# Block-sparse attention with a gated MLP: sums inverted on GpSimd, value products in column halves, K and Q transposed as loaded

## The chip, the cores and the metric

The kernel runs on one core of one Trainium2 chip. The metric is the device time of one execution in microseconds, taken as the median of several runs. The engines are TensorE (PE in the profile, with PEld for its weight loads), VectorE (DVE), ScalarE (ACT), GpSimd (POOL) and SyncE (SP), which issues DMAs.

## The reference

q, k and v have 4 batches, 8 heads, 768 positions and a head size of 64. Positions form 24 blocks of 32. A query block sees itself and its two neighbours, the first and the last block, and three sampled blocks; the first and the last query block see everything.

```python
scores = scale * np.matmul(q, k.transpose(0, 1, 3, 2))
mask = np.abs(blk_i - blk_j) <= window              # window = 1
mask = mask | (blk_i == 0) | (blk_j == 0) | (blk_i == n_blocks - 1) | (blk_j == n_blocks - 1)
# and the three sampled blocks of each query block
scores = np.where(mask, scores, -1000000000.0)
scores = scores - np.max(scores, axis=-1, keepdims=True)
attn = np.exp(scores)
attn = attn / (np.sum(attn, axis=-1, keepdims=True) + 1e-09)
x = np.matmul(attn, v)                              # heads side by side: 3072 tokens x 512
h = x @ w_in                                        # 512 -> 2048
g = h * (1.0 / (1.0 + np.exp(-beta * h)))
out = g @ w_out                                     # 2048 -> 512
```

## The kernel before

**A planner sets the order.** The kernel adds tasks, each with an engine (or several to choose from), an expected duration, dependences and a priority. `plan.run()` plays them through at build time, hands out the eight PSUM banks, and gives one order. The instructions are emitted in it, so each engine works its own list in order, with semaphores between engines. A task with a choice, such as `nrm` with `{"POOL": 1.85, "DVE": 0.8}`, goes where the planner expects it to end first; a bias keeps `nrm` and `gn` mostly on GpSimd.

**Loading.** For batch 0, SyncE loads K, Q and V in float32 and VectorE casts K and Q (L397). For batches 1 to 3, GpSimd issues the loads, which cast on the way, into two raw buffers `RAW`; a raw partition holds six positions for every head, (head, position, dim). VectorE then copies them (`perm`, L447) into (position, head, dim): `K16`, `Q16` and `Vn`. V goes on to a table in DRAM (`VT`), from which the sampled blocks' rows are gathered.

**Transposing.** `trK` and `trQ` (L463) transpose 128x128 pieces, two heads at a time, into a PSUM bank, six for a pair of heads. `evK` and `evQ` copy the bank to `KT` and `QT`: 128 partitions are two heads of 64 dims.

**Pairs of query blocks.** 44 pairs (11 for each batch) go through: `kg` on GpSimd gathers the sampled key blocks (L521), `kn` copies the neighbours on GpSimd or VectorE, `sc` makes the scores of all heads in two banks (L600 for the mask, L610), in tiles of 64 rows by 32 columns of the array; `mx` finds the maxima (VectorE, L621), `ex` the exponentials and their sums (ScalarE, L629). `rc` inverts the four sums (VectorE, L635), `nrm` multiplies (mostly GpSimd, L641), `tp` transposes the weights (L653), `ptv` copies them out (L657), `av` multiplies by the values (L668), and two `xv` tasks copy the result to `xT`.

`av` multiplies two heads' values, 128 columns, with the weights of both heads, 64 columns:

```python
nc.tensor.matmul(
    o[:, (g * NHP + hp) * 64:(g * NHP + hp + 1) * 64],
    lhsT=vgb[:, g, c, hp * P:(hp + 1) * P],
    rhs=pt[:, g, c, :, hp * BLK:(hp + 1) * BLK], ...)
```

So half of each product crosses heads and is not used. Each `xv` takes the useful part of one half: 64 partitions, for the head that stands in them.

**Global rows.** The first and last query blocks of a batch go through similar steps in four rounds: `gs`, `gm`, `ge`, `gr` (sum and reciprocal on VectorE, L733 and L734), `gn` (multiply, L737), `gt`, `gptv`, and then one `gav` for all (L758) with two `gx` copies.

**The MLP.** Eight groups of tokens follow the attention as their blocks come ready: `h` (L817), `tanh` (L823), `stt` (L828), `y` (L845), `oe` (L263) and the store. The planner fills TensorE's gaps with them; after the last pair only MLP work is left.

Of the kernel before, what the change touches and what calls it, by code (L numbers as in the profile page):

```python
# [10 lines left out]
FP32 = mybir.dt.float32  # L11
# [3 lines left out]
ALU = mybir.AluOpType  # L15
# [167 lines left out]
def kernel(  # L183
# [16 lines left out]
    P = 128  # L200
# [20 lines left out]
    ones = sb("ones", [P, P])  # L221
    maskr = sb("maskr", [P, NB - 2, 4])
# [8 lines left out]
    K16 = sb("K16", [P, J, D_MODEL])  # L231
    Q16 = sb("Q16", [P, J, D_MODEL])
    RAW = [sb(f"RAW{i}", [P, H, J * D]) for i in range(2)]
# [33 lines left out]


# [3 lines left out]
    def emit_ident():  # L272
        make_identity(nc, identity)
        nc.gpsimd.memset(ones, 1.0)
    t_ident = add("ident", "POOL", 2.0, emit_ident, prio=-100)
# [110 lines left out]
    for i, (nm, t, dst) in enumerate((("K", k, K16), ("Q", q, Q16), ("V", v, None))):  # L386
        for f in range(2):
            tl = add(f"ld{nm}0.{f}", "SP", 0.47, lambda i=i, t=t, f=f: nc.sync.dma_start(
                out=stage_half(i, f) if i < 2 else v_stage[:, f * HH:(f + 1) * HH, :],
                in_=src6(t, 0, f * HH, HH)), prio=-80 + i * 2 + f, dma=2.0, hw=1)  # L390
            if nm == "V":
                v0ld.append(tl)
                continue
            for hp in range(2 * f, 2 * f + 2):
                ld[nm, 0, hp] = add(
                    f"cast{nm}0.{hp}", "DVE", 0.5,
                    lambda i=i, dst=dst, hp=hp: nc.vector.tensor_copy(  # L397
                        out=dst[:, :, hp * P:(hp + 1) * P].rearrange("p j (h d) -> p h j d", h=2),
                        in_=stage32(i, hp).rearrange("p h (j d) -> p h j d", j=J)),
                    deps=[tl], prio=-72 + 4 * i + hp)  # L400
# [30 lines left out]
    trK, trQ, evK, evQ, vperm, vtab, perm = {}, {}, {}, {}, {}, {}, {}  # L431
    later = {b: [] for b in range(B)}
    for b in range(B):
        pr = prep_prio(b)
        if b:
            vperm[b] = []
            for nm, t, raw, dst in (("V", v, RAW[0], Vn[b % 2]), ("K", k, RAW[1], K16), ("Q", q, RAW[0], Q16)):
                tr = {"K": trK, "Q": trQ}.get(nm)
                for f in range(2):
                    hs = slice(f * HH, (f + 1) * HH)  # L440
                    free = [vperm[b][f]] if nm == "Q" else [perm["QK"["VK".index(nm)], b - 1, f]] if b > 1 else []
                    tl = add(f"ld{nm}{b}.{f}", "POOL", 0.9, lambda t=t, raw=raw, b=b, f=f, hs=hs:
                             nc.gpsimd.dma_start(out=raw[:, hs, :], in_=src6(t, b, f * HH, HH)),
                             deps=free + [t_wout[-1]] if b == 1 else free,
                             prio=(-40 if b == 1 else pr - 30) + "VKQ".index(nm) + 0.5 * f, dma=2.55, bulk=THR)
                    later[b].append(tl)
                    tpm = add(f"perm{nm}{b}.{f}", "DVE", 0.55, lambda raw=raw, dst=dst, hs=hs: copy_on(  # L447
                        "DVE", dst[:, :, hs.start * D:hs.stop * D].rearrange("p j (h d) -> p h j d", h=HH),
                        raw[:, hs, :].rearrange("p h (j d) -> p h j d", j=J)),
                        deps=[tl] + ([tr[b - 1, hp] for hp in range(2 * f, 2 * f + 2)] if tr else []),  # L450
                        prio=pr - 5 * (nm == "V"))
                    if nm == "V":
                        vperm[b].append(tpm)
                    else:
                        perm[nm, b, f] = tpm
                        for hp in range(2 * f, 2 * f + 2):
                            ld[nm, b, hp] = tpm
        for nm, s16, dstT, tr, ev in (("K", K16, KT, trK, evK), ("Q", Q16, QT, trQ, evQ)):
            for hp in range(NHP):
                def emit_tr(nm=nm, s16=s16, b=b, hp=hp):  # L460
                    o = bank16((nm, b, hp))
                    for j in range(J):
                        nc.tensor.transpose(  # L463
                            out=o[:, j * P:(j + 1) * P],
                            in_=s16[:, j, hp * P:(hp + 1) * P],
                            identity=identity)
# [36 lines left out]
    for n, (b, p) in enumerate(order_pairs):  # L503
# [116 lines left out]
        for u in range(2):  # L620
# [14 lines left out]
        rc = add(f"rc{n}", "DVE", 0.09, lambda sb_=sb_: nc.vector.reciprocal(  # L635
            out=sb_[:, 2, :], in_=sb_[:, 1, :]), deps=[ex[n, 0], ex[n, 1]], prio=pr)

        def emit_nrm(eng, pb=pb, sb_=sb_):
            for u in range(2):
                for g in range(2):  # L640
                    (nc.vector if eng == "DVE" else nc.gpsimd).tensor_scalar(  # L641
                        out=pb[:, u, g, :], in0=pb[:, u, g, :],
                        scalar1=sb_[:, 2, 2 * u + g:2 * u + g + 1], scalar2=1.0,
                        op0=ALU.mult, op1=ALU.mult)
        nrm[n] = add(f"nrm{n}", {"POOL": 1.85, "DVE": 0.8}, None, emit_nrm, deps=[rc], prio=pr - 0.5)
# [15 lines left out]
        def emit_av(n=n, vgb=vgb):  # L661
            o = bank(("O", n))
            pt = PT[n % NPT].rearrange("x (g c u m) -> x g c u m", g=2, c=2, u=2)
            first = True
            for g in range(2):
                for hp in range(NHP):
                    for c in range(2):
                        nc.tensor.matmul(  # L668
                            o[:, (g * NHP + hp) * 64:(g * NHP + hp + 1) * 64],
                            lhsT=vgb[:, g, c, hp * P:(hp + 1) * P],  # L670
                            rhs=pt[:, g, c, :, hp * BLK:(hp + 1) * BLK],
                            start=first, stop=(c == 1), skip_group_check=True)
                        first = False
        av[n] = add(f"av{n}", "PE", 0.47, emit_av, deps=[ptv[n], vres] + vg[n], prio=pr - 0.5, lat=0.2,
                    opens=(("O", n),))
        evs = []
        for u in range(2):
            def emit_xv(eng, n=n, u=u, b=b, i0=i0):
                src = bank(("O", n))[u * D:(u + 1) * D, :].rearrange(
                    "x (g h v m) -> x g h v m", g=2, h=NHP, v=2)[:, :, :, u, :]  # L680
                c0 = x_of(b * NB + i0)
                dst = xT[u * D:(u + 1) * D, :, c0:c0 + 2 * BLK].rearrange(
                    "x h (g m) -> x g h m", g=2)
                copy_on(eng, dst, src)
            evs.append(add(f"xv{n}.{u}", {"DVE": 0.42, "ACT": 0.38}, None, emit_xv, deps=[av[n]], prio=pr - 0.5,
                           closes=(("O", n),)))
# [7 lines left out]
    for b in range(B):  # L694
        for w, (blk, u) in enumerate((bl, u) for bl in (0, NB - 1) for u in range(2)):
# [36 lines left out]
            def emit_gr(s_=s_):  # L732
                nc.vector.tensor_reduce(out=s_[:, 5:6], in_=s_[:, 3:5], axis=AX.X, op=ALU.add)  # L733
                nc.vector.reciprocal(out=s_[:, 6:7], in_=s_[:, 5:6])  # L734
            gr = add(f"gr{m}", "DVE", 0.26, emit_gr, deps=[ge], prio=pr)
            gn[m] = add(f"gn{m}", {"POOL": 0.9, "DVE": 0.44}, None, lambda eng, s_=s_, pg=pg: (
                nc.vector if eng == "DVE" else nc.gpsimd).tensor_scalar(  # L737
                out=pg, in0=pg, scalar1=s_[:, 6:7], scalar2=1.0, op0=ALU.mult, op1=ALU.mult),
                deps=[gr], prio=pr)
# [13 lines left out]
        def emit_gav(b=b):  # L753
            o = bank(("GO", b))
            first = True
            for hp in range(NHP):
                for j in range(J):
                    nc.tensor.matmul(  # L758
                        o[:, hp * P:(hp + 1) * P], lhsT=Vn[b % 2][:, j, hp * P:(hp + 1) * P],
                        rhs=PTG[:, j, :, hp * BLK:(hp + 1) * BLK],  # L760
                        start=first, stop=(j == J - 1), skip_group_check=True)
                    first = False
        gavt[b] = add(f"gav{b}", "PE", 1.4, emit_gav, deps=[gptv[gun - 4 + w] for w in range(4)] +
                      vperm[b], prio=pr, lat=0.2, opens=(("GO", b),))
        evs = []
        for u in range(2):
            def emit_gx(eng, u=u, b=b):
                src = bank(("GO", b))[u * D:(u + 1) * D, :].rearrange(
                    "x (h k v m) -> x h k v m", h=NHP, k=2, v=2)
                for kk, blk in enumerate((0, NB - 1)):  # L770
                    c0 = x_of(b * NB + blk)
                    dst = xT[u * D:(u + 1) * D, :, c0:c0 + BLK]
                    copy_on(eng, dst, src[:, :, kk, u, :])
            evs.append(add(f"gx{b}.{u}", {"DVE": 0.55, "ACT": 0.5}, None, emit_gx, deps=[gavt[b]], prio=pr,
                           closes=(("GO", b),)))
# [128 lines left out]
```

## Time and profile before

| | |
|---|---|
| median of 3 runs (lowest to highest) | 323.93 us (323.91 to 328.18) |
| profiled execution, its own time | 323.59 us |
| its span | 321.8 us, 10665 instructions |
| mean granted clock | 0.929 of full |
| PE busy | 280.7 us (87%) in 3525 matmuls |
| PEld busy | 177.3 us (55%) |
| DVE busy | 246.7 us (77%) in 572 instructions |
| ACT busy | 216.8 us (67%) in 644 |
| POOL busy | 187.5 us (58%) in 528 |
| DMA | 43.97 MB in 42211 packets |

The span runs from the first to the last instruction that the profiler saw, and the execution's own time has 1.8 us more. Busy time is the sum over an engine's instructions; for PE the ends of matmuls are modelled, so the distance between two starts tells more than a duration. In a row of a group stand line, engine, operation, output and input with shapes, the count, then busy us and mean ns of one, then the idle time of the engine before them and what ended it.

### The profile page before, as it was taken

What the parts mean: (1) busy time and instruction counts of PE and PEld (TensorE: products, weight loads), DVE (VectorE), ACT (ScalarE), POOL (GpSimd) and SP (SyncE); (2) the same over time, 40 slices, a digit from 0 to 9 for tenths busy, and PEclk for the clock granted to TensorE, in tenths of its full rate; (3) what the DMA queues carried; (4) which work ended last, traced back from release to release, by engine and by line L of the source; (5) the groups of instructions that cost most, each with busy time, mean ns of one, the idle gap of its engine ahead of it and who ended that gap; (6) DMA issues with size and microseconds to landing.
All of it is one profiled execution on the core that took longest, in us unless ns stands there. A gap on an engine that the chain in (4) does not pass through costs nothing.

```text
span 321.8 us, 10665 instructions
## 1 busy us (share of the span) xinstructions
PE 280.7 (87%) x3525; PEld 177.3 (55%) x3525; DVE 246.7 (77%) x572; ACT 216.8 (67%) x644; POOL 187.5 (58%) x528
## 2 busy tenths in 40 slices
PE   0845578989979699988979999999999999999994
PEld 0612366956755486556635656555665555554671
DVE  2996579878869989999987667999979975771060
ACT  1676435864968489789687669977679864772361
POOL 2479956848778456798966654756948453200000
PEclk9975557999979989999979999999999999999999
DMA  7889995998697586323777973335232333100201
GB/s 255 332 172 208 229 227 105 187 252 177 132 204 145 164 212 114 107 80 94 125 146 168 226 170 93 88 84 153 94 118 69 91 110 100 33 3 33 98 2 66
DMA packets 42211, 43.97 MB, mean 137 GB/s; under 512 B 6440, under 2 KB 37672, under 8 KB 42156
## 3 DMA queue, kind: packets, MB, share of 16 engines
q1 hardware_dynamic: 27760, 25.71, 27.1%
q0 software_dynamic: 10784, 11.27, 23.4%
q10 hardware_dynamic: 3612, 6.30, 5.4%
q8 instruction: 28, 0.46, 0.6%
q14 instruction: 27, 0.22, 0.2%
HBM read 45.10 MB, written 9.44 MB: 169 GB/s over the span
## 4 chain that ended last, share of the span: by engine, by line
PE 60%; DMA 14%; DVE 12%; ACT 6%; issue 3%; SPq 3%; POOL 1%; POOLq 0%; ACTq 0%; DVEq 0%
PE bank L845 22%; PE bank L817 21%; DMA VG<-VT 6%; PE bank L668 4%; PE bank L653 4%; DMA RAW<-in_k_dram 3%; DMA VT<-Vn 3%; SPq L582 3%; DVE ST L621 2%; ACT PP L629 2%; PE bank L463 2%; DVE g L828 2%; PE bank L610 2%; PE bank L600 2%; DMA sbl<-in_sampled_blocks_dram 1%
## 5 line engine op out<-in xcount | busy, mean ns | idle before, releaser
L641 POOL TENSOR_SCALAR PP<-PP,ST 128x256 f16<-128x256 f16 x168 | 81.3, 501 | 47.9 <-DVE ST L635 42.4
L629 ACT ACTIVATE PP<-bank,ST 128x256 f16<-128x256 f32 x176 | 81.6, 478 | 30.1 <-DVE ST L621 21.5
L817 PE MATMUL bank<-xT,w_in_sb 128*128 128x256 f16 (+1 forms) x512 | 97.1, 338 | 3.9 <-ACT PP L629 1.1
L845 PE MATMUL bank<-w_out_sb,g 128*128 128x512 f16 x384 | 90.9, 380 | 0.0
L828 DVE SCALAR_TENSOR_TENSOR g<-t,bank 128x512 f16<-128x512 f16 (+1 forms) x128 | 66.6, 546 | 22.1 <-ACT t L823 21.3
L823 ACT ACTIVATE t<-bank,beta_sb 128x512 f16<-128x512 f32 (+1 forms) x128 | 69.9, 589 | 14.3 <-PE bank L817 11.6
L817 PEld LDWEIGHTS <-w_in_sb 128*128 128x128 f16 x512 | 55.3, 116 | 30.1 <-issue 8.6
L521 POOL COPY KG<-KT 128x64 f32 x264 | 54.6, 256 | 24.6 <-PE bank L610 17.8
L621 DVE TENSOR_REDUCE ST<-bank 128x2 f32<-128x512 f32 x88 | 57.5, 678 | 7.5 <-PE bank L610 7.4
L845 PEld LDWEIGHTS <-g 128*128 128x128 f16 x384 | 34.7, 98 | 38.6 <-issue 4.1
L668 PE MATMUL bank<-PT,VG 128*128 128x64 f16 x704 | 31.8, 199 | 7.9 <-DMA VG<-VT 5.9
L668 PEld LDWEIGHTS <-VG 128*128 128x128 f16 x704 | 28.3, 102 | 16.5 <-issue 9.6
L629 ACT ACTIVATION_READ_ACCUMULATOR PP<-bank,ST 128x1 f32 x176 | 36.8, 209 | 0.0
L653 PE MATMUL bank<-identity,PP 128*128 128x128 f16 x352 | 30.9, 233 | 6.6 <-ACT xT L257 2.4
L653 PEld LDWEIGHTS <-PP 128*128 128x128 f16 x352 | 24.6, 104 | 15.9 <-issue 4.1
L657 DVE COPY PT<-bank 128x1024 f16<-128x1024 f16 x44 | 30.1, 684 | 4.1 <-PE bank L653 3.3
L259 DVE CAST xT<-bank 64x256 f16<-64x256 f32 (+1 forms) x52 | 20.6, 402 | 12.3 <-PE bank L668 7.5
L263 ACT ACTIVATE osb<-bank 128x512 f32<-128x512 f32 x24 | 14.4, 601 | 20.7 <-PE bank L845 20.7
L257 ACT CAST xT<-bank 64x256 f16<-64x256 f32 (+1 forms) x52 | 17.4, 346 | 15.4 <-DVE xT L259 6.3
L610 PE MATMUL bank<-KG,QT 64*32 64x256 f16 x704 | 20.9, 293 | 1.4 <-POOL KG L521 1.0
L726 ACT ACTIVATE PG<-bank,SG 128x384 f16<-128x384 f32 x32 | 18.4, 583 | 4.9 <-DVE SG L721 4.1
L600 PE MATMUL bank<-maskr,ones 64*32 64x192 f16 (+1 forms) x352 | 14.9, 272 | 5.7 <-ACT PP L629 5.5
(79 smaller groups left out, 256.6 us busy)
## 6 DMA issues: line engine op xcount, KB each, us to landing
VG<-VT SPq DMA_DIRECT2D x268, 32.0 KB, 2.6
VG<-VT SPq DMA_DIRECT2D x40, 192.0 KB, 2.9
out_dram<-osb ACTq DMA_DIRECT2D x20, 256.0 KB, 2.2
RAW<-in_v_dram POOLq DMA_DIRECT2D x6, 384.0 KB, 5.1
RAW<-in_k_dram POOLq DMA_DIRECT2D x6, 384.0 KB, 5.6
VT<-Vn SPq DMA_DIRECT2D x3, 768.0 KB, 6.1
RAW<-in_q_dram POOLq DMA_DIRECT2D x6, 384.0 KB, 6.5
w_in_sb<-in_moe_w_in_dram POOLq DMA_DIRECT2D x8, 256.0 KB, 5.9
```

What stands on the lines that cost most here:

```text
L521: nc.gpsimd.tensor_copy(out=kg32[:, g, :, (2 + r) * W:(3 + r) * W], in_=kt32[:, :, bass.ds(vals[3 * g + r], W)])
L610: nc.tensor.matmul(bk[u][hp * BLK:(hp + 1) * BLK, g * 256:(g + 1) * 256], lhsT=QT[b % 2][u * D:(u + 1) * D, hp, (i0 + g) * BLK:(i0 + g + 1 ...
L621: mx[n, u] = add(f"mx{n}.{u}", "DVE", 0.6, lambda n=n, u=u, sb_=sb_: nc.vector.tensor_reduce(out=sb_[:, 0, 2 * u:2 * u + 2], in_=bank(("S" ...
L629: nc.scalar.activation(out=pb[:, u, g, :], in_=bank(("S", n, u))[:, g * 256:(g + 1) * 256], func=AF.Exp, bias=sb_[:, 0, 2 * u + g:2 * u + ...
L641: (nc.vector if eng == "DVE" else nc.gpsimd).tensor_scalar(out=pb[:, u, g, :], in0=pb[:, u, g, :], scalar1=sb_[:, 2, 2 * u + g:2 * u + g + ...
L653: nc.tensor.transpose(out=o[:, s * P:(s + 1) * P], in_=pb[:, u, g, c * P:(c + 1) * P], identity=identity)
L657: ptv[n] = add(f"ptv{n}", "DVE", 0.61, lambda n=n: nc.vector.tensor_copy(out=PT[n % NPT], in_=bank16(("T", n))), deps=[tp[n]] + ([av[n - N ...
L668: nc.tensor.matmul(o[:, (g * NHP + hp) * 64:(g * NHP + hp + 1) * 64], lhsT=vgb[:, g, c, hp * P:(hp + 1) * P], rhs=pt[:, g, c, :, hp * BLK: ...
L817: nc.tensor.matmul(o[:, 0:TW], lhsT=w_in_v[:, c, f // 4, f % 4, :], rhs=xT[:, c, c0:c0 + TW], start=(c == 0), stop=(c == NHP - 1))
L823: lambda G=G, f=f, TW=TW, tt=tt: nc.scalar.activation(out=tt[:, 0:TW], in_=bank(("H", G, f))[:, 0:TW], func=AF.Tanh, bias=0.0, scale=beta_ ...
L828: lambda G=G, f=f, TW=TW, tt=tt, gg=gg: nc.vector.scalar_tensor_tensor(out=gg[:, f, 0:TW], in0=tt[:, 0:TW], scalar=1.0, in1=bank(("H", G, ...
L845: nc.tensor.matmul(o[:, :], lhsT=gg[:, f, s * P:(s + 1) * P], rhs=w_out_sb[:, f, :], start=(f == 0), stop=(f == N_FFC - 1))
```

## The change

The invert, the sums and the multiply become one task on the engine that multiplies; on GpSimd the inverse is a power of -1. The raw K and Q are transposed directly, one head at a time, into halves of the partitions, and `perm` stays for V alone. `av` and `gav` are written as two products per pair of heads, each 64 columns of the array wide, so that the useful part of the output is dense; one `xv` and one `gx` copy all 128 partitions. The global rounds take the last block before the first, so that both lie side by side in `xT`. The diff, cut to its core:

```diff
+    minus = sb("minus", [P, 4], FP32)
...
-    K16 = sb("K16", [P, J, D_MODEL])
-    Q16 = sb("Q16", [P, J, D_MODEL])
-    RAW = [sb(f"RAW{i}", [P, H, J * D]) for i in range(2)]
+    RK, RQ, RV = (sb(f"R{x}", [P, H, J * D]) for x in "KQV")
...
+    def invert_on(eng, out, in_, n):
+        if eng == "DVE":
+            nc.vector.reciprocal(out=out, in_=in_)
+        else:
+            nc.gpsimd.tensor_tensor(out=out, in0=in_, in1=minus[:, 0:n], op=ALU.pow)
...
-                        out=dst[:, :, hp * P:(hp + 1) * P].rearrange("p j (h d) -> p h j d", h=2),
-                        in_=stage32(i, hp).rearrange("p h (j d) -> p h j d", j=J)),
+                        out=dst[:, 2 * hp:2 * hp + 2, :], in_=stage32(i, hp)),
...
-                    free = [vperm[b][f]] if nm == "Q" else [perm["QK"["VK".index(nm)], b - 1, f]] if b > 1 else []
+                    hps = range(2 * f, 2 * f + 2)
+                    if tr is None:
+                        free = [vperm[b - 1][f]] if b > 1 else []
+                    else:
+                        free = [tr[b - 1, hp] for hp in hps]
...
-                    tpm = add(f"perm{nm}{b}.{f}", "DVE", 0.55, lambda raw=raw, dst=dst, hs=hs: copy_on(
...
                     else:
-                        perm[nm, b, f] = tpm
-                        for hp in range(2 * f, 2 * f + 2):
-                            ld[nm, b, hp] = tpm
+                        for hp in hps:
+                            ld[nm, b, hp] = tl
...
                     for j in range(J):
-                        nc.tensor.transpose(
-                            out=o[:, j * P:(j + 1) * P],
-                            in_=s16[:, j, hp * P:(hp + 1) * P],
-                            identity=identity)
+                        for u in range(2):
+                            nc.tensor.transpose(
+                                out=o[u * D:(u + 1) * D, j * P:(j + 1) * P],
+                                in_=s16[:, 2 * hp + u, j * D:(j + 1) * D],
+                                identity=identity, tile_position=(0, u * D))
...
-        rc = add(f"rc{n}", "DVE", 0.09, lambda sb_=sb_: nc.vector.reciprocal(
-            out=sb_[:, 2, :], in_=sb_[:, 1, :]), deps=[ex[n, 0], ex[n, 1]], prio=pr)
-
         def emit_nrm(eng, pb=pb, sb_=sb_):
+            invert_on(eng, sb_[:, 2, :], sb_[:, 1, :], 4)
...
-        nrm[n] = add(f"nrm{n}", {"POOL": 1.85, "DVE": 0.8}, None, emit_nrm, deps=[rc], prio=pr - 0.5)
+        nrm[n] = add(f"nrm{n}", {"POOL": 2.0, "DVE": 0.9}, None, emit_nrm, deps=[ex[n, 0], ex[n, 1]], prio=pr - 0.5)
...
                     for c in range(2):
-                        nc.tensor.matmul(
-                            o[:, (g * NHP + hp) * 64:(g * NHP + hp + 1) * 64],
-                            lhsT=vgb[:, g, c, hp * P:(hp + 1) * P],
-                            rhs=pt[:, g, c, :, hp * BLK:(hp + 1) * BLK],
-                            start=first, stop=(c == 1), skip_group_check=True)
-                        first = False
+                        for u in range(2):
+                            us = slice(u * D, (u + 1) * D)
+                            nc.tensor.matmul(
+                                o[us, (g * NHP + hp) * BLK:(g * NHP + hp + 1) * BLK],
+                                lhsT=vgb[:, g, c, (2 * hp + u) * D:(2 * hp + u + 1) * D],
+                                rhs=pt[:, g, c, u, hp * BLK:(hp + 1) * BLK],
+                                start=(g + hp + c == 0), stop=(c == 1), skip_group_check=True,
+                                tile_position=(0, u * D))
...
+        def emit_xv(eng, n=n, b=b, i0=i0):
+            c0 = x_of(b * NB + i0)
+            copy_on(eng, xT[:, :, c0:c0 + 2 * BLK].rearrange("x h (g m) -> x g h m", g=2),
+                    bank(("O", n))[:, 0:2 * NHP * BLK].rearrange("x (g h m) -> x g h m", g=2, h=NHP))
+        evs = [add(f"xv{n}", {"DVE": 0.42, "ACT": 0.38}, None, emit_xv, deps=[av[n]], prio=pr - 0.5,
+                   closes=(("O", n),))]
...
-        for w, (blk, u) in enumerate((bl, u) for bl in (0, NB - 1) for u in range(2)):
+        for w, (blk, u) in enumerate((bl, u) for bl in (NB - 1, 0) for u in range(2)):
...
-            def emit_gr(s_=s_):
-                nc.vector.tensor_reduce(out=s_[:, 5:6], in_=s_[:, 3:5], axis=AX.X, op=ALU.add)
-                nc.vector.reciprocal(out=s_[:, 6:7], in_=s_[:, 5:6])
-            gr = add(f"gr{m}", "DVE", 0.26, emit_gr, deps=[ge], prio=pr)
...
+            def emit_gn(eng, s_=s_, pg=pg):
+                E = nc.vector if eng == "DVE" else nc.gpsimd
+                E.tensor_tensor(out=s_[:, 5:6], in0=s_[:, 3:4], in1=s_[:, 4:5], op=ALU.add)
+                invert_on(eng, s_[:, 6:7], s_[:, 5:6], 1)
+                E.tensor_scalar(out=pg, in0=pg, scalar1=s_[:, 6:7], scalar2=1.0, op0=ALU.mult, op1=ALU.mult)
+            gn[m] = add(f"gn{m}", {"POOL": 1.15, "DVE": 0.65}, None, emit_gn, deps=[ge], prio=pr)
...
                 for j in range(J):
-                    nc.tensor.matmul(
-                        o[:, hp * P:(hp + 1) * P], lhsT=Vn[b % 2][:, j, hp * P:(hp + 1) * P],
-                        rhs=PTG[:, j, :, hp * BLK:(hp + 1) * BLK],
-                        start=first, stop=(j == J - 1), skip_group_check=True)
+                    for u in range(2):
+
+                        nc.tensor.matmul(
+                            o[u * D:(u + 1) * D, hp * 2 * BLK:(hp + 1) * 2 * BLK],
+                            lhsT=Vn[b % 2][:, j, (2 * hp + u) * D:(2 * hp + u + 1) * D],
+                            rhs=PTG[:, j, u::2, hp * BLK:(hp + 1) * BLK],
+                            start=(hp + j == 0), stop=(j == J - 1), skip_group_check=True,
+                            tile_position=(0, u * D))
...
+        evs = [add(f"gx{b}", {"DVE": 0.42, "ACT": 0.38}, None, emit_gx, deps=[gavt[b]], prio=pr,
+                   closes=(("GO", b),))]
```

With the planned durations changed so, the planner's order and its choices of engine change too.

More of the change, by code (lines that the diff above doesn't have):

```diff
@@ L274, in emit_ident @@
         nc.gpsimd.memset(ones, 1.0)
+        nc.gpsimd.memset(minus, -1.0)
     t_ident = add("ident", "POOL", 2.0, emit_ident, prio=-100)
@@ L385 @@
     v0ld = []
-    for i, (nm, t, dst) in enumerate((("K", k, K16), ("Q", q, Q16), ("V", v, None))):
+    for i, (nm, t, dst) in enumerate((("K", k, RK), ("Q", q, RQ), ("V", v, None))):
         for f in range(2):
@@ L429, in prep_prio @@
         return -50 if b == 0 else 10 * (NPAIR * (b - 1) + 4)
[L431 removed]
+    trK, trQ, evK, evQ, vperm, vtab = {}, {}, {}, {}, {}, {}
     later = {b: [] for b in range(B)}
@@ L436 @@
             vperm[b] = []
-            for nm, t, raw, dst in (("V", v, RAW[0], Vn[b % 2]), ("K", k, RAW[1], K16), ("Q", q, RAW[0], Q16)):
+            for nm, t, raw in (("V", v, RV), ("K", k, RK), ("Q", q, RQ)):
                 tr = {"K": trK, "Q": trQ}.get(nm)
@@ L446 @@
                     later[b].append(tl)
-                    tpm = add(f"perm{nm}{b}.{f}", "DVE", 0.55, lambda raw=raw, dst=dst, hs=hs: copy_on(
[L448 to L451, printed above, removed]
                     if nm == "V":
-                        vperm[b].append(tpm)
-                    else:
-                        perm[nm, b, f] = tpm
-                        for hp in range(2 * f, 2 * f + 2):
-                            ld[nm, b, hp] = tpm
-        for nm, s16, dstT, tr, ev in (("K", K16, KT, trK, evK), ("Q", Q16, QT, trQ, evQ)):
+                        vperm[b].append(add(f"permV{b}.{f}", "DVE", 0.55, lambda b=b, hs=hs: copy_on(
+                            "DVE", Vn[b % 2][:, :, hs.start * D:hs.stop * D].rearrange("p j (h d) -> p h j d", h=HH),
+                            RV[:, hs, :].rearrange("p h (j d) -> p h j d", j=J)), deps=[tl], prio=pr - 5))
+                    else:
+                        for hp in hps:
+                            ld[nm, b, hp] = tl
+        for nm, s16, dstT, tr, ev in (("K", RK, KT, trK, evK), ("Q", RQ, QT, trQ, evQ)):
             for hp in range(NHP):
@@ L663, in emit_av @@
             pt = PT[n % NPT].rearrange("x (g c u m) -> x g c u m", g=2, c=2, u=2)
-            first = True
             for g in range(2):
@@ L667, in emit_av @@
                     for c in range(2):
-                        nc.tensor.matmul(
-                            o[:, (g * NHP + hp) * 64:(g * NHP + hp + 1) * 64],
-                            lhsT=vgb[:, g, c, hp * P:(hp + 1) * P],
-                            rhs=pt[:, g, c, :, hp * BLK:(hp + 1) * BLK],
-                            start=first, stop=(c == 1), skip_group_check=True)
-                        first = False
+                        for u in range(2):
[6 more added lines that the diff above has]
+                                tile_position=(0, u * D))
         av[n] = add(f"av{n}", "PE", 0.47, emit_av, deps=[ptv[n], vres] + vg[n], prio=pr - 0.5, lat=0.2,
                     opens=(("O", n),))
[L676 to L686, printed above, removed]
+        def emit_xv(eng, n=n, b=b, i0=i0):
[4 more added lines that the diff above has]
+                   closes=(("O", n),))]
         for g in range(2):
@@ L730 @@
                      closes=(("GS", m, 0), ("GS", m, 1)))
-            def emit_gr(s_=s_):
-                nc.vector.tensor_reduce(out=s_[:, 5:6], in_=s_[:, 3:5], axis=AX.X, op=ALU.add)
-                nc.vector.reciprocal(out=s_[:, 6:7], in_=s_[:, 5:6])
-            gr = add(f"gr{m}", "DVE", 0.26, emit_gr, deps=[ge], prio=pr)
[L736 to L739, printed above, removed]
+            def emit_gn(eng, s_=s_, pg=pg):
[4 more added lines that the diff above has]
+            gn[m] = add(f"gn{m}", {"POOL": 1.15, "DVE": 0.65}, None, emit_gn, deps=[ge], prio=pr)
             def emit_gt(m=m, pg=pg):
@@ L754, in emit_gav, with emit_gx @@
             o = bank(("GO", b))
-            first = True
             for hp in range(NHP):
                 for j in range(J):
-                    nc.tensor.matmul(
-                        o[:, hp * P:(hp + 1) * P], lhsT=Vn[b % 2][:, j, hp * P:(hp + 1) * P],
-                        rhs=PTG[:, j, :, hp * BLK:(hp + 1) * BLK],
-                        start=first, stop=(j == J - 1), skip_group_check=True)
-                    first = False
+                    for u in range(2):
[5 more added lines that the diff above has]
+                            tile_position=(0, u * D))
         gavt[b] = add(f"gav{b}", "PE", 1.4, emit_gav, deps=[gptv[gun - 4 + w] for w in range(4)] +
                       vperm[b], prio=pr, lat=0.2, opens=(("GO", b),))
[L765 to L775, printed above, removed]
+        def emit_gx(eng, b=b):
+            c0 = x_of(b * NB + NB - 1)
+            copy_on(eng, xT[:, :, c0:c0 + 2 * BLK],
+                    bank(("GO", b))[:, 0:2 * NHP * BLK].rearrange("x (h m) -> x h m", h=NHP))
+        evs = [add(f"gx{b}", {"DVE": 0.42, "ACT": 0.38}, None, emit_gx, deps=[gavt[b]], prio=pr,
+                   closes=(("GO", b),))]
         for blk in (0, NB - 1):
```

## The prediction

> **What bounds the kernel now.** I read the page, then the busy time by stage, then TensorE's order of time, the waits, and last the groups by line with shapes kept apart. Busy time in three stretches (the columns: PE, PEld, DVE, ACT, POOL busy us with instruction counts, granted clock, DMA share, GB/s):
>
> ```profile
> 0.00:60.00 60.00, 35.51 (x496) 24.45 (x497) 44.73 (x128) 31.46 (x102) 40.05 (x116) 0.72 0.90 222
> 60.00:160.00 100.00, 90.29 (x1336) 64.00 (x1334) 89.06 (x212) 76.75 (x242) 75.48 (x203) 0.97 0.68 149
> 160.00:322.00 162.00, 154.94 (x1698) 88.83 (x1695) 112.88 (x235) 108.63 (x303) 72.00 (x211) 0.98 0.37 97
> ```
>
> The first 60 us are the start: loads, the V table written and gathered back, DMA share 0.90, TensorE half empty. From 60 to 160 PE and VectorE are both near 90. From 160 on PE has nearly all, VectorE 70%. A busy PE is not a PE at its peak, so I took the starts of its matmuls from the trace and counted as idle what lies beyond the streaming time of each (216 ns for 512 columns, 56 for 128, 29 for 64 at full clock, each the usual distance of two starts) and beyond the changes of tile shape shown next: idle 24.7 us in the first stretch, 13.4 in the second (so 86.6 needed), 3.5 in the third. After 160 us each us added to TensorE is a us of the span.
>
> TensorE in order of time:
>
> ```profile
> 200.40 0.63 PE L668 MATMUL bank<-PT,VG 128*128 128x64 f16 x16
> 200.96 0.28 PE L600 MATMUL bank<-maskr,ones 64*32 64x192 f16 x8
> ...
> 205.40 0.28 PE L600 MATMUL bank<-maskr,ones 64*32 64x192 f16 x8
> 205.50 0.40 PE L610 MATMUL bank<-KG,QT 64*32 64x256 f16 x16
> 205.83 0.64 PE L668 MATMUL bank<-PT,VG 128*128 128x64 f16 x16
> 206.31 1.03 PE L817 MATMUL bank<-xT,w_in_sb 128*128 128x512 f16 x4
> ```
>
> Two things stand in the starts. The value products (L668) take 0.48 us to the next start (205.83 to 206.31, 29 ns each) if full-array work follows, but 0.56 if L600 follows, whose tiles are 64x32: a change of tile shape costs 0.09 us. The records put it at 93 ns each way, at every place where no wait covers it; the order has 88 of them. And matmuls on different 64x32 tiles run side by side: L610's 16 matmuls of 256 columns (107 ns each) fit in 0.33 us with a shape change included.
>
> The costs by line that the change touches:
>
> ```profile
> L641 POOL TENSOR_SCALAR PP<-PP,ST 128x256 f16<-128x256 f16 x168 | 81.3, 501 | 47.9 <-DVE ST L635 42.4 <-ACT KT L257 4.1 <-ACT t L823 1.2
> L668 PE MATMUL bank<-PT,VG 128*128 128x64 f16 x704 | 31.8, 199 | 7.9 <-DMA VG<-VT 5.9 <-DVE PT L657 1.9
> L259 DVE CAST xT<-bank 64x256 f16<-64x256 f32 x46 | 19.2, 418 | 11.8 <-PE bank L668 7.5 <-ACT xT L257 3.7
> L257 ACT CAST xT<-bank 64x256 f16<-64x256 f32 x42 | 15.4, 366 | 15.4 <-DVE xT L259 6.3 <-PE bank L668 6.0 <-DMA out_dram<-osb 2.8
> L635 DVE RECIPROCAL ST<-ST 128x4 f32<-128x4 f32 x44 | 7.4, 169 | 4.1 <-ACT PP L629 3.8
> L259 DVE COPY K<-RAW 128x1536 f16<-128x1536 f16 x6 | 5.4, 897 | 1.8 <-DMA RAW<-in_k_dram 1.8
> L259 DVE COPY Q<-RAW 128x1536 f16<-128x1536 f16 x6 | 3.7, 610 | 2.5 <-DMA RAW<-in_q_dram 2.5
> ```
>
> GpSimd stood idle 42.4 us for the reciprocal alone. One case in order of time:
>
> ```profile
> 134.53 0.21 ACT L629 ACTIVATION_READ_ACCUMULATOR PP<-bank,ST 128x1 f32 x1
> 135.85 0.17 DVE L635 RECIPROCAL ST<-ST 128x4 f32<-128x4 f32 x1
> 136.12 1.85 POOL L641 TENSOR_SCALAR PP<-PP,ST 128x256 f16<-128x256 f16 x4 [1.47 <-DVE ST L635]
> ```
>
> The sums are ready at 134.74; VectorE, in order, comes to the reciprocal 1.11 us later. Over pairs 6 to 22 (the second stretch) that delay is 1.4 us in the mean, after that mostly 0.03 to 0.3.
>
> **The change part by part.**
>
> *Inversion.* On VectorE 42 of 44 reciprocals go (42 x 0.169 = 7.1 us), and of the global rows' sums and reciprocals 12 of 16 (3.6 us with the rest's extra). GpSimd gets 42 powers of 128x4 and 12 times an add and a power of 128x1. No row shows a power. The nearest rows are GpSimd's few-element ops: 0.24 us (66 elements multiplied) below, 0.92 (768 elements, L737) above, the latter for a power computed in many steps. I take 0.4, nearer the low end since there are only four elements a partition. Each next multiply waits for GpSimd's own write, as at L305 to L307 (0.09 us). So 0.49 us stands against the reciprocal's 0.17, a hop of 0.1 and the queueing: per pair about +1.2 us of latency saved in the second stretch, nothing later. In all GpSimd gets 42 x 0.49 + 12 x 0.6 = 28 us and gives up 9 (15 neighbour copies, 2 value copies, a multiply): 187.5 to 206 busy. Behind the waiting power on GpSimd stand gathers (L521) and DMA issues, as now behind L641. The Trainium skill (GPSIMD Engine Reference, § Engine selection) has GpSimd about half as fast as VectorE in elementwise work of two inputs; by that the power is an estimated 0.34 us, if it costs like an add, and the sum moves by nothing that shows.
>
> *x copied at once.* 52 copies on VectorE become 19, 52 on ScalarE 28. Each covers 128 partitions instead of 64 with the same 256 columns, so at the old price (0.42, 0.37): 12.7 us off VectorE, 7.2 off ScalarE.
>
> *K and Q transposed as loaded.* The 12 rearrangements go: 9.1 us off VectorE, 6 us of it in the second stretch, and with them a step between load and transpose. The loads into own buffers now wait for the transposes of the batch before; the first such issue is at 90.3 us and the transposes it needs ended at 73.1, so nothing; without that cover the gathers behind the DMA issue would wait. The first casts read and write straight rows: 0.54 us at most, as now.
>
> *What comes back.* The planner gives VectorE 15 more neighbour copies (0.4 each, 6 us), 2 more value copies, 2 more KT evictions, one more multiply (3.4 us). VectorE: 246.7 - 32.5 + 9.4 = 224; its second stretch from 89 to some 76.
>
> *TensorE.* Value products: 704 of 64 columns become 1408 of 32 in 128x64 tiles, two halves side by side. No row shows that shape. If the halves overlap, 16 pairs cost at least 16 ns (29 and 56 ns for 64 and 128 columns put 32 columns at 16), and if loading weights bounds them as it may now, 29; if they don't, 32 x 29. So 0.25 to 0.93 us per group of today's 0.47; I take 0.47, since different tiles did overlap in L610. Transposes of K and Q: 12 halves at 56 per pair, as 6 now: nothing. Global products: 24 x 56 = 1.34 become 24 x 29 = 0.70, -0.64 each. But all these groups now have a shape of their own: 190 changes in the order instead of 88. By stretches 7, 51 and 44 more at 93 ns: 0.65, 4.7, 4.1 us.
>
> **Sum.** First stretch: the DMAs set it; 5 powers on a GpSimd that is full from 20 to 40 us: +1.0 (-2 to +3). Second: needed 86.6 + 4.7 - 1.3 = 90.0; idle 13.4 falls to 7, as VectorE goes from 89 to 76 and the reciprocal's delay goes: 97.0, so -3.0. Third: +4.1 - 0.64 = +3.5, with no idle to hide it. Together +1.5 on 321.8: 323.3; 1.8 us lie around the span (323.59 in all), so 325.1, and the median of the runs was 0.34 above that one: 325.4.
>
> **The rivals.** *The halves' weights load one after the other* (slower). 1408 loads instead of 704, 29 ns for each matmul with its load as in L668: each group 0.93 us, the global one 48 x 29 = 1.39; the transposes hide it (two loads within 56 ns). Third stretch +22 x 0.467 + 0.7 = +11.0; second +9.3, of which 4 fill idle time: 342. Each ns over 29 per pair costs 16 x 22 = 0.35 us after 160 and half of 16 x 17 before, 0.49 us together: from 39 ns a pair on the loss is over 2%. For it: twice the loads, and no row with 128 rows and 64 columns. Against it: the side-by-side starts in L600 and L610. The Trainium skill (TensorEngine Tiling, § Restrictions and Gotchas) says that column tiling shuts off the fast weight load; the trace here shows 128 full weights hidden behind 64 columns, and no half. That speaks for this rival.
>
> *The power is slow* (slower). GpSimd has some 60 us free between 20 and 278 us, 1.5 us per pair, so from about 1.9 us a power it is the bound; at 2.5 it adds 42 x 0.6 = 25: 350. Nothing in the trace speaks against it but the price of other small ops.
>
> *The relief is worth more* (faster). Halves at 16 ns a pair (-0.21 per group: -4.7 third, -3.6 second, -1 first) and idle in the second stretch down to 4: 313. For it: VectorE's queue is behind most of the second stretch's delays. Against: the last 160 us hardly wait for VectorE.
>
> **How the numbers follow.** Forecast 0.38 (its own range 318 to 333: 0.28 within 2%, 0.08 above, 0.02 below), weights in turn 0.25, slow power 0.09, more relief 0.28 (0.26 below 2%, 0.02 within). So faster by over 2% 0.28, within 0.30, slower 0.42; 2% is about what a measurement of this kernel tells from no change. The range, 311 to 346, leaves out a slow power's far side and the tail below the relief.
>
> **What would show it.** Right: value groups that take 0.47 us plus 0.09 at each border; a power of 0.3 to 0.6 us within 0.1 us of ScalarE's last sum; VectorE below 230 us busy; PE idle after 60 us below 12. Wrong: the 32 halves take 0.9 us (weights); GpSimd's busy time above 240; or a second stretch as long as before, which would say that VectorE's queue was not its bound.

## The result, and the profile after

The changed kernel is slower: 340.4 us in the median of four runs against 326.1 for the kernel before beside it, 1.052 times as long (95% interval 1.043 to 1.062). The forecast was 325.4 with a range of 311 to 346; the time lies in the range, on the side to which the text gave 0.42, and 15 us from the point. The profiled execution took 340.43 us, its span 338.7. Some executions of any kernel here run a few per cent longer than its others, and the ratios leave those out, so that a ratio is not always that of the medians shown.

Busy time of the changed kernel in the same stretches (us of PE, PEld, DVE, ACT, POOL, then granted clock, DMA share, GB/s):

```profile
0.00:60.00 60.00, 37.40 (x655) 27.36 (x655) 44.83 (x124) 31.75 (x101) 46.36 (x128) 0.72 0.91 216
60.00:160.00 100.00, 88.39 (x1574) 56.71 (x1575) 72.99 (x162) 66.66 (x212) 78.52 (x190) 0.94 0.65 148
160.00:339.00 179.00, 171.19 (x2292) 94.69 (x2291) 108.69 (x196) 110.52 (x306) 105.25 (x260) 0.99 0.36 91
```

VectorE fell as forecast (89 to 73 in the second stretch), but TensorE did not fill the room: it is less busy there than before, and the third stretch is 17 us longer. GpSimd's busy time grew most in that third stretch, from 72 to 105.

The groups by line that answer to those shown of before:

```profile
L645 POOL TENSOR_SCALAR PP<-PP,ST 128x256 f16<-128x256 f16 x168 | 80.1, 494 | 4.2
L271 POOL TENSOR_TENSOR ST<-ST,minus 128x4 f32<-128x4 f32 x42 | 43.7, 1041 | 32.9 <-ACT PP L635 32.8
L271 POOL TENSOR_TENSOR SG<-SG,minus 128x1 f32<-128x1 f32 x12 | 6.7, 558 | 0.9
L673 PE MATMUL bank<-PT,VG 128*64 128x32 f16 x1408 | 33.3, 189 | 3.4 <-DMA VG<-VT 3.4
L256 ACT CAST xT<-bank 128x256 f16<-128x256 f32 x28 | 10.6, 378 | 23.2 <-PE bank L673 20.8
L258 DVE CAST xT<-bank 128x256 f16<-128x256 f32 x20 | 8.4, 422 | 6.4 <-PE bank L673 5.9
```

A power of four columns takes 1.04 us, of one column 0.56. An x copy of 128 partitions costs what one of 64 cost before (0.38 us on ScalarE, 0.42 on VectorE). GpSimd no longer waits for VectorE, but TensorE now waits for GpSimd (the list of waits: engine and line, for whom, us in all, times, longest):

```profile
POOL ST L271 <- ACT PP L635: 32.8, 16, 8.5
...
PEld L657 <- POOL PP L645: 17.0, 34, 2.1
...
PEld L743 <- POOL PG L736: 9.9, 9, 3.4
```

Before, the first of these two waits of the weight loads came to 3.2 us. The chain of work that ended last, by engine, says the same; first the kernel before, then the changed one:

```profile
PE 60%; DMA 14%; DVE 12%; ACT 6%; issue 3%; SPq 3%; POOL 1%; POOLq 0%; ACTq 0%; DVEq 0%
PE 40%; POOL 22%; DMA 13%; DVE 8%; issue 5%; ACT 5%; POOLq 3%; SPq 3%; ACTq 0%; DVEq 0%
```

GpSimd in order of time shows why:

```profile
138.00 1.12 POOL L527 COPY KG<-KT 128x64 f32 x6
139.09 1.01 POOL L271 TENSOR_TENSOR ST<-ST,minus 128x4 f32<-128x4 f32 x1
140.20 1.85 POOL L645 TENSOR_SCALAR PP<-PP,ST 128x256 f16<-128x256 f16 x4
141.99 1.12 POOL L527 COPY KG<-KT 128x64 f32 x6
143.08 1.02 POOL L271 TENSOR_TENSOR ST<-ST,minus 128x4 f32<-128x4 f32 x1
144.19 1.85 POOL L645 TENSOR_SCALAR PP<-PP,ST 128x256 f16<-128x256 f16 x4
146.00 0.19 POOL L734 TENSOR_TENSOR SG<-SG 128x1 f32<-128x1 f32 x1
146.28 0.56 POOL L271 TENSOR_TENSOR SG<-SG,minus 128x1 f32<-128x1 f32 x1
```

Each starts as the one before it ends: a gather, a power, four multiplications, 4 us a pair with no wait in it. By the records GpSimd goes on without a gap over 0.3 us from 125.2 to 164.5 us, for 39 us; after the first 60 us the longest such stretch of the kernel before was 12.5 us. (In the first 60 us the longest were 39 and 19.)

TensorE's side:

```profile
202.37 1.05 PE L812 MATMUL bank<-xT,w_in_sb 128*128 128x512 f16 x4
203.35 0.68 PE L673 MATMUL bank<-PT,VG 128*64 128x32 f16 x32
203.97 1.92 PE L812 MATMUL bank<-xT,w_in_sb 128*128 128x512 f16 x8
```

32 halves take 0.62 us to the next start, a shape change of 0.09 included: 0.53, or 33 ns a pair. Had they gone one after the other at 29 ns, it would be 0.93. The records show the two halves of a pair mostly starting 3 or 4 ns apart, and the pairs 32.

### The profile page after: what moved, and what is told of

Same layout as the page of the kernel before. It is cut to its first block, busy times and chain, and to the rows that moved or that the text cites. A ratio compares the mean times of both kernels' runs of the same rounds, so it can differ in the third digit from the quotient of the medians.

```text
span 338.7 us, 12565 instructions
## 1 busy us (share of the span) xinstructions
PE 297.0 (88%) x4517; PEld 178.8 (53%) x4517; DVE 226.5 (67%) x482; ACT 208.9 (62%) x618; POOL 230.1 (68%) x577
## 4 chain that ended last, share of the span: by engine, by line
PE 40%; POOL 22%; DMA 13%; DVE 8%; issue 5%; ACT 5%; POOLq 3%; SPq 3%; ACTq 0%; DVEq 0%
PE bank L840 15%; PE bank L812 14%; POOL PP L645 8%; DMA VG<-VT 7%; POOL ST L271 6%; POOL KG L527 4%; PE bank L673 3%; ACT PP L635 3%; POOLq L522 3%; SPq L588 3%; PE bank L469 2%; PE bank L657 2%; DVE g L823 2%; DMA VT<-Vn 2%; DMA RQ<-in_q_dram 2%
## 5 line engine op out<-in xcount | busy, mean ns | idle before, releaser
L840 PE MATMUL bank<-w_out_sb,g 128*128 128x512 f16 x384 | 92.2, 380 | 0.1
L645 POOL TENSOR_SCALAR PP<-PP,ST 128x256 f16<-128x256 f16 x168 | 80.1, 494 | 4.2
L627 DVE TENSOR_REDUCE ST<-bank 128x2 f32<-128x512 f32 x88 | 57.4, 683 | 17.7 <-PE bank L616 17.6
L271 POOL TENSOR_TENSOR ST<-ST,minus 128x4 f32<-128x4 f32 x42 | 43.7, 1041 | 32.9 <-ACT PP L635 32.8
L527 POOL COPY KG<-KT 128x64 f32 x264 | 52.6, 248 | 17.2 <-PE bank L616 10.6
L657 PE MATMUL bank<-identity,PP 128*128 128x128 f16 x352 | 34.9, 236 | 10.2 <-POOL PP L645 9.0
L635 ACT ACTIVATION_READ_ACCUMULATOR PP<-bank,ST 128x1 f32 x176 | 38.4, 218 | 0.0
L673 PEld LDWEIGHTS <-VG 128*64 128x64 f16 x1408 | 28.9, 119 | 16.6 <-issue 11.0
L673 PE MATMUL bank<-PT,VG 128*64 128x32 f16 x1408 | 33.3, 189 | 3.4 <-DMA VG<-VT 3.4
L256 ACT CAST xT<-bank 128x256 f16<-128x256 f32 x28 | 10.6, 378 | 23.2 <-PE bank L673 20.8
L743 PE MATMUL bank<-identity,PG 128*128 128x128 f16 x96 | 10.6, 263 | 7.6 <-POOL PG L736 5.9
```

Source lines behind the costliest of these rows:

```text
L271: nc.gpsimd.tensor_tensor(out=out, in0=in_, in1=minus[:, 0:n], op=ALU.pow)
L527: nc.gpsimd.tensor_copy(out=kg32[:, g, :, (2 + r) * W:(3 + r) * W], in_=kt32[:, :, bass.ds(vals[3 * g + r], W)])
L627: mx[n, u] = add(f"mx{n}.{u}", "DVE", 0.6, lambda n=n, u=u, sb_=sb_: nc.vector.tensor_reduce(out=sb_[:, 0, 2 * u:2 * u + 2], in_=bank(("S" ...
L635: nc.scalar.activation(out=pb[:, u, g, :], in_=bank(("S", n, u))[:, g * 256:(g + 1) * 256], func=AF.Exp, bias=sb_[:, 0, 2 * u + g:2 * u + ...
L645: (nc.vector if eng == "DVE" else nc.gpsimd).tensor_scalar(out=pb[:, u, g, :], in0=pb[:, u, g, :], scalar1=sb_[:, 2, 2 * u + g:2 * u + g + ...
L657: nc.tensor.transpose(out=o[:, s * P:(s + 1) * P], in_=pb[:, u, g, c * P:(c + 1) * P], identity=identity)
```

## The experiments

The rival theories: (1) the loss comes from the power on GpSimd; (2) it comes from TensorE's shape changes and halves. Ratios are to the kernel before on the same chip. Its own median differed between chips, from 325 to 332 us, so times of different chips are set side by side only where that is said. Two kernels that ran twice came to nearly the same ratio (1.052 and 1.055, 0.991 twice). A third came to 0.981 on the chip of the 332 and to 0.995 on another; the multiplication and the power alone ran on the chip of the 332 only, so their ratios may be a point too low. PE idle is counted as in the prediction, with 32 ns for a pair of halves; of two tries the table has the second.

| kernel | ratio (95% interval) | POOL busy us | PE idle 60 to 160 us | PE idle after 160 us |
|---|---|---|---|---|
| before | 1 | 187.5 | 13.4 | 3.6 |
| changed | 1.052 (1.043 to 1.062) | 230.1 | 17.7 | 6.5 |
| multiplication in the power's place | 0.983 (0.973 to 0.993) | 190.0 | 7.3 | 3.0 |
| power behind the multiplications | 1.055 (1.049 to 1.062) | 231.9 | 15.2 | 4.4 |
| planner told | 1.028 (1.020 to 1.036) | 156.4 | 11.5 | 5.2 |
| power alone | 1.014 (1.004 to 1.023) | 238.2 | 23.0 | 8.5 |
| power and transposes | 1.035 (1.028 to 1.041) | 233.6 | 19.8 | 10.8 |
| halves alone | 1.024 (1.014 to 1.033) | 185.2 | 11.3 | 5.0 |
| transposes alone | 0.991 (0.984 to 0.997) | 184.6 | 14.3 | 1.9 |

**A multiplication in the power's place.**

```diff
-            nc.gpsimd.tensor_tensor(out=out, in0=in_, in1=minus[:, 0:n], op=ALU.pow)
+            nc.gpsimd.tensor_tensor(out=out, in0=in_, in1=minus[:, 0:n], op=ALU.mult)
```

> The changed kernel with one word changed: the power becomes a multiplication (the sums are multiplied by -1 instead of inverted; every engine keeps its order instruction by instruction). Theory 1 (the power, 1.04 us on GpSimd in every pair's chain, is the loss): the small op falls to 0.2 to 0.3 us, GpSimd to some 195 us busy, and the time to 324 to 330, at most 1% over the kernel before. Theory 2 (the loss is TensorE's: 102 more changes of tile shape at 93 ns and 32 ns per pair of halves): the time stays within 3 us of the changed kernel, 336 to 341.

Measured: 0.983 of the kernel before (327.0 against 331.6 us). This kernel leaves the inversion out: the weights are multiplied by the negated sums. Its groups and waits:

```profile
L271 POOL TENSOR_TENSOR ST<-ST,minus 128x4 f32<-128x4 f32 x42 | 9.8, 233 | 57.0 <-ACT PP L635 56.0 <-PE bank L673 0.9
```

```profile
PEld L657 <- POOL PP L645: 3.2, 4, 1.2
```

The order is that of the changed kernel, instruction by instruction, so what separates the two, beside the chip, is the power's duration: 42 times 0.81 us and 12 times some 0.35 are 38 us of GpSimd. It costs 7 points by the ratios, 1.052 and 0.983 (some 22 us), but 13 us by the two profiled spans (338.7 and 325.7); TensorE's idle time after 60 us in the table, 24.2 and 10.3, fits the 13. TensorE's wait for the pairs' multiplications is back at 3.2 us. Theory 2 is out as the cause of the whole: with all its shape changes this order is no slower than the kernel before.

**The changed kernel again**, as the measure for the next two.

> The changed kernel unaltered, on one chip with the next three, as their measure. Both theories: 1.04 to 1.06 times the kernel before; 42 powers at 1.04 us.

Measured: 1.055 (1.045 to 1.065), powers of 1.04 us.

**The power behind the multiplications.**

```diff
-            nc.gpsimd.tensor_tensor(out=out, in0=in_, in1=minus[:, 0:n], op=ALU.pow)
+            nc.gpsimd.tensor_tensor(out=out, in0=in_, in1=minus[:, 0:n], op=ALU.mult)
...
+            if eng != "DVE":
+                nc.gpsimd.tensor_tensor(out=spare, in0=sb_[:, 1, :], in1=minus, op=ALU.pow)
```

> The changed kernel with the cheap multiplication in the inversion's place, and a real power of the same sums issued behind each pair's four multiplications, into a tile that nobody reads (the sums are multiplied by -1 instead of inverted; the global rows have no power). GpSimd's load is about that of the changed kernel, but a pair's transposes don't wait for the power. Theory 1a (the power costs as a step in each pair's own chain): the time comes near the one without a power, 0.98 to 1.00 of the kernel before. Theory 1b (it costs as load: GpSimd works in clumps without a gap, and what is late is the next gather or multiplication): near the changed kernel, 1.03 to 1.05.

Measured: 1.055 (1.049 to 1.062), the same as the changed kernel beside it. The two small operations of this kernel, and TensorE's wait for the multiplications:

```profile
L651 POOL TENSOR_TENSOR spare<-ST,minus 128x4 f32<-128x4 f32 x42 | 43.3, 1031 | 0.0
...
L272 POOL TENSOR_TENSOR ST<-ST,minus 128x4 f32<-128x4 f32 x42 | 9.5, 226 | 30.8 <-ACT PP L636 30.6
...
PEld L660 <- POOL PP L646: 10.5, 19, 1.6
```

No pair waits for its own power here, and yet the whole loss is there. So theory 1b holds: the power costs as load on an engine that works its list in order, in clumps. What it delays is what stands behind it in that list: the weight loads wait 10.5 us for multiplications, where without a power they waited 3.2. Whether the power stands ahead of or behind a pair's own multiplications does not matter in this order. This kernel leaves the inversion out as the one before it did and works on the same values, so the values are not what made that one fast.

**The planner told.**

```diff
-        nrm[n] = add(f"nrm{n}", {"POOL": 2.0, "DVE": 0.9}, ...
+        nrm[n] = add(f"nrm{n}", {"POOL": 3.15, "DVE": 0.9}, ...
-            gn[m] = add(f"gn{m}", {"POOL": 1.15, "DVE": 0.65}, ...
+            gn[m] = add(f"gn{m}", {"POOL": 1.9, "DVE": 0.65}, ...
```

> The changed kernel with the planner's durations set to the measured ones: 3.15 instead of 2.0 for a pair's inversion and multiplication on GpSimd, 1.9 instead of 1.15 for a global round. If the loss comes from an order made for a 0.15 us power, it shrinks to 1.00 to 1.02 of the kernel before, as neighbour copies and some multiplications move to VectorE; if the power costs wherever it stands, 1.03 to 1.05.

Measured: 1.028 (1.020 to 1.036), between the two. GpSimd keeps few of the pairs, VectorE gets the others:

```profile
L271 POOL TENSOR_TENSOR ST<-ST,minus 128x4 f32<-128x4 f32 x11 | 11.3, 1031 | 24.4 <-ACT PP L635 24.4
```

```profile
L645 DVE TENSOR_SCALAR PP<-PP,ST 128x256 f16<-128x256 f16 x132 | 35.2, 333 | 1.2
```

So, told of the price, the planner wins back about half of the loss. This run changes two things at once, the order and the number of powers (11 pairs for 42), and does not say which of them did it. Nothing of the hoped-for gain is left: VectorE is at 247 us busy again, all that the change had taken off it.

**The power alone**, the inversion of the changed kernel put into the kernel before, pairs and global rows; the diff has the pairs' part.

```diff
-        rc = add(f"rc{n}", "DVE", 0.09, ...
...
         def emit_nrm(eng, pb=pb, sb_=sb_):
+            invert_on(eng, sb_[:, 2, :], sb_[:, 1, :], 4)
```

> The kernel before with the inversion alone moved to GpSimd as a power. Theory 1: slower by 8 to 15 us than the kernel before, GpSimd some 230 us busy, and TensorE's idle time after 60 us up from 17 us to 25 or more. Theory 2: within 4 us of the kernel before, as GpSimd had 1.5 us a pair to spare.

Measured: 1.014 (1.004 to 1.023), less than theory 1 had it in time (5 us in the medians, 336.7 against 331.6), though GpSimd's busy time (238) and TensorE's idle time after 60 us (31.5, from 17) came out as expected. Its own trace speaks for a larger loss than the ratio: 14.5 us more of idle time. One thing that went the other way is the granted clock, 1.00 from 60 to 160 us for 0.97 before, an estimated 3 us (0.03 of these 100). This chip's ratio may be the rest; no run settles it.

**Halves alone**, `av`, `gav`, `xv` and `gx` of the changed kernel in the kernel before, the rest as it was; two tries.

```diff
...
-                            o[:, (g * NHP + hp) * 64:(g * NHP + hp + 1) * 64],
-                            lhsT=vgb[:, g, c, hp * P:(hp + 1) * P],
+                                o[us, (g * NHP + hp) * BLK:(g * NHP + hp + 1) * BLK],
+                                lhsT=vgb[:, g, c, (2 * hp + u) * D:(2 * hp + u + 1) * D],
...
```

> The kernel before with the value products in halves and x copied at once, for pairs and global rows; inversion and transposes as before. Theory 1: within 4 us of the kernel before: some 5 us more of shape changes on TensorE after 160 us against 20 us less of copies on VectorE and ScalarE. Theory 2: slower by 6 to 10 us.

Measured: 333.6 us against 331.6, without an interval: open after this try.

> Halves and single x copies alone, again, as the first try gave no interval: if the shape changes on TensorE (some 8 us in all, 4 of them after 160 us) weigh as the prediction has it, 1.00 to 1.015 of the kernel before; if the relief of VectorE and ScalarE outweighs them, 0.98 to 1.00.

Measured: 1.024 (1.014 to 1.033), above both of the ranges expected. The order has 169 shape changes for 88, and the relief of VectorE (247 to 235 us busy) and ScalarE (217 to 207) does not pay for them. Theory 2 has this part right, for the halves alone.

**Transposes alone**, K and Q transposed as loaded in the kernel before; two tries.

```diff
...
-                            in_=s16[:, j, hp * P:(hp + 1) * P],
-                            identity=identity)
+                                in_=s16[:, 2 * hp + u, j * D:(j + 1) * D],
+                                identity=identity, tile_position=(0, u * D))
```

> The kernel before with K and Q alone transposed as loaded, head by head into halves (12 rearranging copies gone, 9.1 us of VectorE; some 20 more changes of tile shape, 2 us). If the gain of the version with VectorE's inversion came from here: 0.975 to 0.99 of the kernel before. If it came from the relief of all parts together: 0.99 to 1.005.

> Direct transposes alone, again: 0.985 to 0.995 of the kernel before.

Measured: 0.991 both times (0.985 to 0.997 and 0.984 to 0.997). This is the one part of the change that gains by itself, 3 us. By stretches, in the first of the two tries:

```profile
60.00:160.00 100.00, 90.69 (x1464) 63.13 (x1469) 87.58 (x218) 78.15 (x246) 75.20 (x205) 1.00 0.71 156
```

**All but the power**: halves, single copies and direct transposes, with the reciprocal on VectorE as before; two tries.

```diff
+        rc = add(f"rc{n}", "DVE", 0.09, lambda sb_=sb_: nc.vector.reciprocal(
+            out=sb_[:, 2, :], in_=sb_[:, 1, :]), deps=[ex[n, 0], ex[n, 1]], prio=pr)
...
-            invert_on(eng, sb_[:, 2, :], sb_[:, 1, :], 4)
...
```

> The changed kernel with the inversion put back to VectorE as its own task (pairs and global rows), with halves, single x copies and direct transposes kept; the planner makes its order anew. Theory 1: 320 to 328, since VectorE keeps most of its relief (some 25 us less busy than in the kernel before). Theory 2: 333 to 340, since TensorE's shape changes are all still there.

> Halves, single x copies and direct transposes, with the inversion on VectorE, beside its two parts on one chip. If the two parts add: the product of the next two ratios. If the halves pay only when VectorE is relieved of the rearrangements too: 0.975 to 0.985 of the kernel before, below the transposes alone.

Measured: 0.981 (0.970 to 0.993), then 0.995 (0.986 to 1.003). Putting the inversion back takes away the loss, and theory 2 is out once more. The two tries do not say whether this is better than the transposes alone at 0.991. They do say that the parts don't add: on the chip of the second try the halves alone had 1.024 and the transposes alone 0.991, a product of 1.015, above the interval of both together, which has 181 shape changes. So the loss that the halves have by themselves hardly shows beside the transposes. Nor is this kernel slower than the order with the cheap multiplication on GpSimd (0.983 on the chip of the first try): an inversion taken off VectorE's queue, even when it costs next to nothing on GpSimd, brought no gain that shows.

**The power with the transposes, without halves.**

> The power and the direct transposes without the halves, to see what makes the power dear in the changed kernel (7 points between its order with the power and with a multiplication, against 1.4 points for the power alone). If the power and the halves hurt each other (shape changes leave TensorE no slack to wait for GpSimd): the parts here add, 1.000 to 1.010 of the kernel before. If a VectorE relieved of the rearrangements only brings GpSimd's clumps forward: 1.02 to 1.04.

Measured: 1.035 (1.028 to 1.041), 1.044 times the transposes alone. The halves are not what makes the power dear: without them it costs 4.4 points here, more than the 1.4 that it cost alone on another chip. That a relieved VectorE brings GpSimd's clumps forward is not shown: the longest stretch of GpSimd without a gap over 0.3 us is 53 us here and 64 with the power alone.

What stays open: the power costs 1.4 points in one order, 4.4 in another, 7 in a third, for nearly the same 40 us of GpSimd. Part of this may be the chips, as said above. Each kernel has an order of its own from the planner, and no run here separates the order's share from the load's. Neither GpSimd's longest stretch without a gap nor TensorE's idle time ranks these losses: the power alone has the most of both (64 and 31.5 us) and the smallest loss.

## Why the prediction was right or wrong

The time lies in the range, but by luck more than by mechanism. The forecast was no change; the range was wide, and of the 0.42 on the slower side only 0.09 stood on the slow power that did it. Of the four signs of being right, the value groups and VectorE's busy time came true; the power's duration and TensorE's idle time after 60 us (24.2 for below 12) did not. GpSimd, at 230 us, stayed below the 240 that should have given a slow power away.

- **The power: the term that failed.** It was taken at 0.4 us between 0.24 and 0.92; it took 1.04, above the upper bound, and the sum gave the load on GpSimd no cost after 60 us. The bound was a row of a multiplication over 768 columns, and no multiplication says how long a power computes. The two sizes in the profile (0.56 us for 128x1, 1.04 for 128x4) would make it an estimated 0.16 us a column on 0.40.
- **The slow power as a rival: right mechanism, wrong threshold.** The text let it decide from 1.9 us on, from 60 us of spare time shared out over 42 pairs. It decided at 1.04. The spare time was not spread evenly over the pairs: before the change GpSimd was free for 9.3 of the 20 us from 180 to 200, but for 1.2 of the 20 from 140 to 160, and in the changed kernel the 39 us without a gap lie across that place. The chance of 0.09 followed from that threshold.
- **Latency saved by leaving VectorE's queue: partly.** With the multiplication in its place idle time from 60 to 160 us fell to 7.3, the forecast had 7. With the power it rose to 17.7. That relief is not the inversion's alone, as putting it back on VectorE gave 0.981 to 0.995.
- **Shape changes: right in number and price.** 190 against 88, at 93 ns. The halves alone have 81 more changes, 7.5 us at that price, and lose 2.4 points, some 8 us; but with the direct transposes 93 more changes (8.6 us) come with no loss that shows (0.981 to 0.995). The Trainium skill (TensorEngine Tiling, § Tiling Modes) says that a change of tiling mode drains TensorE; the trace agrees, and prices it.
- **Halves overlap: right.** 32 ns a pair against the 29 taken; the rival with weights loaded one after the other (58 ns, 342 us) did not happen, though its time is near the measured one. The Trainium skill's remark (TensorEngine Tiling, § Restrictions and Gotchas) that column tiling has no fast weight load can account here for the 3 ns a pair between 29 and 32 at most.
- **Global products, x copies, rearrangements: right.** 48 halves at some 16 ns each are 0.77 us to the last start for 1.28 before; copies of 128 partitions cost the same as of 64; VectorE came to 226.5 us for the 224 of the sum.
- **The sum.** With the cheap multiplication the order's span was 325.7 us, against 323.3 in the forecast's sum, but on the chip where the kernel before took 332 us. By the ratio it is 0.983, where the forecast was 1.005 (325.4 to 323.9) and the rival of more relief 0.966 (313). So without the power the rest came out between the forecast and that rival, within some 2 points of the sum, and the power turned it into a loss.

## What to carry to other kernels

Spare time of an in-order engine, averaged over the span, is no slack: look for the stretches without a gap and for who waits behind them. They warn of a loss; they did not tell its size here. An operation that no row shows has no upper bound from rows of other operations: give the rival that it is several times dearer a real chance, or time it by itself first. Replacing one operation by a cheap one in an unchanged order separates its price from everything else in a change of many parts.

## What the runs showed of the hardware

- A GpSimd power of 128x4 in float32 takes 1.03 to 1.05 us in the mean of each run, of 128x1 0.56 to 0.59; a multiplication of 128x4 takes 0.23. VectorE's reciprocal of 128x4 took 0.17.
- A change of TensorE's tile shape costs 93 ns each way, between 128x64 and full tiles as between 64x32 and full ones.
- Two 128x64 halves run side by side, 32 ns a pair with new weights for each and 32 columns.
- TensorE's granted clock in the second stretch was 0.94 in the changed kernel, 0.97 with the multiplication in the power's place and 1.00 with the power alone, which has the most idle time there (23.0 us). So idle time by itself does not set it, and no run here shows what does.
